# Issuing a kernel's first four loads between SyncE's arrival at the opening barrier and its wait there

## The chip, the cores and the metric

The kernel runs on one core of one Trainium2 chip. The metric is device time in microseconds (us) of one execution. A kernel is executed several times; a run is called slow when it lies over 1.5% above the fastest of the same kernel, and only fast runs are compared.

Two numbers are close but not the same. The *time* is what is compared. The *span* of a profile goes from the first to the last instruction that the profile shows.

## The reference

One decode step: conditioned layer norm, grouped-query attention over a cache of 8192 keys, then a gated MLP. Nearly all its bytes are weights and caches that are read once.

```python
# B=8, D=1024, Hq=32, Hkv=4, Sk=8192, Dh=128, F=3584, bfloat16
mod = silu(c) @ w_mod                     # (8, 6*1024): sa, ca, ga, sb, cb, gb
h = layernorm(x) * (1 + ca) + sa
x = x + ga * attention(h, k_cache, v_cache, wq, wo)
h = layernorm(x) * (1 + cb) + sb
x = x + gb * ((relu(h @ W_gate) * (h @ W_up)) @ W_down)
```

## The kernel before

All big operands pass through one ring in SBUF, the `arena`. A list of loads, in the order of use, is worked off by SyncE (SP in the profile); a load waits only until its part of the ring has been read by its last reader. Operations are recorded first and then emitted engine by engine, with a semaphore wait wherever another engine's result is needed.

```python
def pump():
    while stream:
        key, src, n = stream[0]
        lo = cursor[0] if cursor[0] + n <= RING else 0
        if P.unread("arena", lo, lo + n):
            return
        # ... (cut)
        P.op("sp", lambda e, dst=dst, src=src: e.dma_start(dst, src), writes=[slot_r(lo, lo + n)], dma=True)
# ... (cut)
for i in range(2):
    load(("wm", i), wm_src[:, 24 * D * i:24 * D * (i + 1)], 24 * D)        # w_mod, 2 x 6 MB
for i in range(2):
    load(("wq", i), wq_src[:, 2 * i * SLOT:2 * (i + 1) * SLOT], 2 * SLOT)  # 2 x 4 MB
for m in range(M):                                                         # 16 x (k, v), 4 MB each
    # ... (cut)
# ... then wo, W_gate and W_up, W_down in five parts, the last of 256 KB (cut)
head = stream[1:]
del stream[1:]
pump()                                     # load 1: first half of w_mod
for t, src in enumerate((c..., A_x...)):   # loads 2 and 3: c and x, 16 KB each (cut)
    P.op("sp", lambda e, t=t, src=src: e.dma_start(cx[:, t, :], src), writes=[R("cx", t, t + 1)], dma=True)
stream.extend(head)
P.pump = pump
pump()                                     # load 4: second half of w_mod; load 5: first half of wq; ...
```

The program opens with a barrier that the kernel's author did not write. Each of ACT, PE, DVE and SP has an instruction that signals its arrival and, right behind it, one that waits for the release. POOL first writes four constants, then waits for the four arrivals and releases everybody. All of the kernel's own instructions, loads too, come behind it.

## Time and profile before

| | before |
|---|---|
| time, median of the first 3 runs | 439.22 us (439.19 to 439.45) |
| time, mean of all 40 fast runs seen in this study | 439.52 us |
| share of the DMA engines' time that the loads take | 98.4% |
| first load issued after SP's arrival at the barrier | 0.74 us |

From the page of the kernel before: the span, the DMA engines' busy tenths in 40 equal slices, what they moved, three of the queues (packets, MB, share of 16 engines), the first being that of the loads, and the chain that ended last, by engine.

```profile
span 438.7 us, 4012 instructions
...
DMA  8999999999999999999999999999999999999994
GB/s 359 433 421 444 436 433 429 434 430 429 430 433 430 429 430 430 432 436 434 436 432 433 445 432 430 430 430 432 430 429 428 430 432 437 434 430 430 431 425 180
...
q1 hardware_dynamic: 6896, 185.64, 98.4%
q8 instruction: 13, 0.21, 0.2%
q14 instruction: 5, 0.04, 0.0%
...
PE 35%; DMA 32%; DVE 26%; ACT 4%; issue 2%; SPq 1%
...
```

The DMA row and the queue's 98.4% say that the DMA engines are the bound: they are at nine tenths or more in every slice but the first and the last, at about 430 GB/s. The last line must not be read as a list of costs. It is a walk back from the end, at each step to what released it; where a load waited on SP for its ring slot, the walk goes on through the matmul that freed it, however long the load then stood in the DMA queue.

The first 3 us of the timeline (columns: start, duration, engine, source line, operation, output and input):

```profile
...
0.34 0.10 POOL L641 MEMSET const-uint8-127<- 128x1 uint8 x1
0.73 1.28 ACT L292 ACT_TABLE_LOAD   x1 [0.73 <-PEq L641]
0.73 0.20 POOL L276 MEMSET identf<- 128x128 f32 x1 [0.29 <-POOLq L641]
0.74 0.40 SPq L237 DMA_DIRECT2D arena<-in_w_mod_dram  x1
...
1.19 0.42 SPq L266 DMA_DIRECT2D cx<-in_c_dram  x1
...
1.66 0.41 SPq L266 DMA_DIRECT2D cx<-in_A_x_dram  x1
...
2.11 0.67 SPq L237 DMA_DIRECT2D arena<-in_w_mod_dram  x1
2.82 0.51 SPq L237 DMA_DIRECT2D arena<-in_A_wq_dram  x1
```

Four constants of POOL, then the barrier, then everything else at once at 0.73 us: ACT loads its table, POOL goes on, and SP issues the first load at 0.74 us. A single row of "DMA_DIRECT2D" is the *issue* of a load, 0.4 us on SP's side, not its data. The Trainium skill says so ("Perfetto Trace Analysis", DMA Instruction — HWDGE): the movement of the data is not in the instruction's profiled window. The trace agrees: the issue is over at 1.14 us, the first packet of the load starts at 1.76 us and the load has landed at 18.5 us.

The instructions that the profile does not count as busy are in the trace as well. Here is the barrier, from the records of the trace (start and duration in us):

```
0.000 0.007 SP    arrives              0.534 0.017 POOL has all four arrivals
0.116 0.010 DVE   arrives              0.612 0.017 POOL releases
0.132 0.008 ACT   arrives              0.654 0.017 SP   passes
0.304 0.186 POOL  finishes constants   0.658 0.017 ACT  passes
0.316 0.008 PE    arrives              0.736 0.403 SP   issues load 1
```

SP is the first to arrive and has 0.65 us of waiting before it. What SP waited for in the whole program (total us, times, longest):

```profile
...
engine line waited for: us in total, times, longest us
SPq L237 <- PE ps L482: 201.6, 16, 13.3
...
SPq L641 <- PEq L641: 0.7, 1, 0.7
```

The barrier is the last line, 0.7 us. (The view puts it down to PE. In the records PE is the last of the four to arrive, and POOL, busy with its constants until 0.49 us, is the one that releases.) The other waits of loads (the longest is shown) are for ring slots; they are long, but loads already in the queue keep the DMA engines busy through them.

The end of the timeline: the last matmuls, the first of the two last DVE operations, SP's two stores:

```profile
...
434.86 1.02 PE L610 MATMUL ps<-arena,kt 128*32 128x256 bf16 x12 [0.18 <-DMA arena<-in_B_W_down_dram]
...
435.93 0.42 DVE L614 TENSOR_TENSOR lu<-ps,mod 128x256 f32<-128x256 f32 x1 [12.25 <-PE ps L610]
...
436.84 0.71 SPq L621 DMA_DIRECT2D out_dram<-ob  x2
...
```

### The profile page before, as it was taken

The page shows a single profiled execution, that of the slowest core. Times are in us where ns is not written, and L with a number is a line of the kernel's source. Part 1 is how long each engine was busy: PE and PEld are TensorE (multiplying, and loading weights), DVE is VectorE, ACT ScalarE, POOL GpSimd, SP SyncE. Part 2 cuts the span into 40 slices and gives each one's busy share as a digit, 9 for nine tenths or more (in the row PEclk, how much of TensorE's full clock was granted, in tenths as well). Part 3 has the DMA queues.
Part 4 walks back from the last instruction along what each step waited for, and adds up shares of the span by engine and source line. Part 5 has one row for each costly group of instructions (what it writes and reads, how often), then busy time and mean ns, then how long its engine had stood idle before and what let it go on. Part 6 is the DMA issues. An engine that isn't in the chain of part 4 may idle for free.

```text
span 438.7 us, 4012 instructions
## 1 busy us (share of the span) xinstructions
PE 271.6 (62%) x1691; PEld 121.2 (28%) x1691; DVE 263.6 (60%) x372; ACT 28.8 (7%) x48; POOL 19.8 (5%) x77
## 2 busy tenths in 40 slices
PE   0053446759595866859586776859586685655243
PEld 0021112324242332324233332424233242342021
DVE  0143057787687867778596867869687878430020
ACT  1100012010101011010101001010101101100000
POOL 6000010000000000000000000000000000000000
PEclk9997669697888969698796968888798978685556
DMA  8999999999999999999999999999999999999994
GB/s 359 433 421 444 436 433 429 434 430 429 430 433 430 429 430 430 432 436 434 436 432 433 445 432 430 430 430 432 430 429 428 430 432 437 434 430 430 431 425 180
DMA packets 6946, 185.90 MB, mean 424 GB/s; under 512 B 816, under 2 KB 912, under 8 KB 1168
## 3 DMA queue, kind: packets, MB, share of 16 engines
q1 hardware_dynamic: 6896, 185.64, 98.4%
q8 instruction: 13, 0.21, 0.2%
q14 instruction: 5, 0.04, 0.0%
q10 hardware_dynamic: 32, 0.01, 0.0%
HBM read 185.63 MB, written 0.02 MB: 423 GB/s over the span
## 4 chain that ended last, share of the span: by engine, by line
PE 35%; DMA 32%; DVE 26%; ACT 4%; issue 2%; SPq 1%
PE ps L482 18%; DMA arena<-in_A_k_cache_dram 15%; PE ps L439 13%; DVE kt L428 10%; DMA arena<-in_A_wq_dram 9%; DMA arena<-in_B_W_down_dram 8%; DVE pT L473 7%; DVE negm L446 4%; ACT prb L466 4%; PE ps L452 1%; PE ps L571 1%; DVE mj L457 1%; PE ps L375 1%; PE ps L592 1%; DVE mjt L460 1%
## 5 line engine op out<-in xcount | busy, mean ns | idle before, releaser
L428 DVE STREAM_TRANSPOSE kt<-arena 128x1024 uint32<-128x1024 uint32 x128 | 149.1, 1215 | 40.4 <-DMA arena<-in_A_k_cache_dram 33.1
L439 PE MATMUL ps<-kt,qpad 128*128 128x512 bf16 x512 | 120.8, 382 | 10.0 <-DVE kt L428 8.7
L482 PE MATMUL ps<-arena,pT 128*64 128x512 bf16 x512 | 94.0, 547 | 51.1 <-DVE pT L473 51.1
L482 PEld LDWEIGHTS ps<-arena,pT 128*64 128x64 bf16 x512 | 44.8, 155 | 94.5 <-issue 89.7
L439 PEld LDWEIGHTS ps<-kt,qpad 128*128 128x128 bf16 x512 | 45.5, 97 | 83.7 <-DVE kt L428 26.5
L473 DVE STREAM_TRANSPOSE pT<-prb 64x1024 bf16<-64x1024 bf16 x32 | 39.6, 1239 | 15.9 <-ACT prb L466 15.4
L466 ACT ACTIVATE prb<-ps,bias 128x1024 bf16<-128x1024 f32 x16 | 17.8, 1113 | 275.0 <-DVE mjt L460 275.0
L446 DVE TENSOR_REDUCE negm<-ps 128x1 f32<-128x512 f32 x32 | 22.1, 689 | 11.7 <-PE ps L439 11.7
L421 POOL COPY qpad<-qR 32x32 bf16<-32x32 bf16 x64 | 13.0, 203 | 308.2 <-PE ps L439 253.8
L592 PE MATMUL ps<-arena,hT 128*32 128x448 bf16 x128 | 12.7, 577 | 14.5 <-DMA arena<-in_B_W_up_dram 6.8
L452 PE MATMUL ps<-identf,negm 128*128 128x128 f32 x32 | 7.8, 325 | 15.7 <-DVE negm L450 15.7
L495 DVE SCALAR_TENSOR_TENSOR om<-ps,im,om 128x128 f32<-128x128 f32 x48 | 16.7, 347 | 0.6
L599 DVE TENSOR_TENSOR kt<-ps,kt 128x448 bf16<-128x448 f32 x2 | 1.2, 619 | 25.0 <-PE ps L592 25.0
L500 PE MATMUL ps<-jmp,om 128*128 128x16 f32 x32 | 6.5, 279 | 14.7 <-DVE om L495 14.7
L375 PE MATMUL ps<-arena,hT 128*32 128x512 bf16 x64 | 6.9, 608 | 13.9 <-DMA arena<-in_A_wq_dram 13.9
L290 DVE CAST cxr<-ps 128x512 bf16<-128x512 f32 x1 | 0.7, 692 | 19.6 <-PE ps L288 19.6
L288 PE MATMUL ps<-cx,rsel 32*128 32x512 bf16 x1 | 0.6, 581 | 19.0 <-DMA cx<-in_A_x_dram 19.0
L610 PE MATMUL ps<-arena,kt 128*32 128x256 bf16 x112 | 6.0, 372 | 9.2 <-DMA arena<-in_B_W_down_dram 9.2
L452 PEld LDWEIGHTS ps<-identf,negm 128*128 128x128 f32 x32 | 4.7, 186 | 23.6 <-DVE negm L450 22.1
L385 DVE CAST kt<-ps 128x512 bf16<-128x512 f32 x1 | 0.7, 692 | 17.2 <-PE ps L375 17.2
L592 PEld LDWEIGHTS ps<-arena,hT 128*32 128x32 bf16 x128 | 4.5, 139 | 22.0 <-DMA arena<-in_B_W_up_dram 8.4
L500 PEld LDWEIGHTS ps<-jmp,om 128*128 128x128 f32 x32 | 5.0, 195 | 18.0 <-DVE om L495 16.9
(80 smaller groups left out, 94.7 us busy)
## 6 DMA issues: line engine op xcount, KB each, us to landing
arena<-in_A_k_cache_dram SPq DMA_DIRECT2D x16, 4096.0 KB, 28.2
arena<-in_A_v_cache_dram SPq DMA_DIRECT2D x16, 4096.0 KB, 25.1
arena<-in_w_mod_dram SPq DMA_DIRECT2D x2, 6144.0 KB, 17.8
arena<-in_A_wq_dram SPq DMA_DIRECT2D x2, 4096.0 KB, 20.0
arena<-in_A_wo_dram SPq DMA_DIRECT2D x2, 4096.0 KB, 26.9
arena<-in_B_W_gate_dram SPq DMA_DIRECT2D x2, 3584.0 KB, 29.4
arena<-in_B_W_up_dram SPq DMA_DIRECT2D x2, 3584.0 KB, 32.5
arena<-in_B_W_down_dram SPq DMA_DIRECT2D x1, 3584.0 KB, 36.0
```

Source lines behind the costliest of these rows:

```text
L375: fns.append(lambda e, w=w, z=z, g=g, kk=kk: e.matmul(ps[32 * g:32 * g + 32, 3 + z, :], hT[:, kk, :], w[:, g, z, :], start=(kk == 0), stop ...
L421: P.op("pool", lambda e, n=2 * m + Q // 2, Q=Q: e.tensor_copy(qpad[32 * Q:32 * Q + 32, m % 2, :, 24 + 32 * Q:32 + 32 * Q], qR[32 * Q:32 * ...
L428: P.op("dve", lambda e: e.transpose(ktb[:, to:to + QE].bitcast(dt.uint32), arena[:, lo:lo + QE].bitcast(dt.uint32)), reads=[slot_r(lo, lo ...
L439: fns.append(lambda e, t=t, r=r: e.matmul(ps[:, b, :].rearrange("p (c k) -> p c k", k=32), qpad[:, m % 2, t * 2 + r, 24 - 8 * i:152 - 8 * ...
L446: P.op("dve", lambda e: e.tensor_reduce(negm[:, h:h + 1], ps[:, b, :], AX.X, ALU.max, negate=True), reads=[bank(b)], writes=[R("negm", h, ...
L452: P.op("pe", lambda e: e.matmul(ps[:, 4, 0:128], negm[:, 2:3].to_broadcast([128, 128]), identf[:], start=True, stop=True), reads=[R("negm" ...
L466: P.op("act", lambda e: e.activation(prb[:], ps[:, 2 * z:2 * z + 2, :].rearrange("p h n -> p (h n)"), ACT.Exp, bias=bias[:, z:z + 1], scal ...
L473: P.op("dve", lambda e, g=g: e.transpose(pT[64 * g:64 * g + 64, z, :, g, :], prb[64 * g:64 * g + 64, :]), reads=[R("prb"), R("pT", z, z + ...
L482: fns.append(lambda e, t=t: e.matmul(ps[64 * (t % 2):64 * (t % 2) + 64, 5, :].rearrange("p (i d) -> p i d", d=Dh), pT[:, z, t].rearrange(" ...
L495: P.op("dve", lambda e, i=i: e.scalar_tensor_tensor(out=om[:], in0=ps[:, 5, Dh * i:Dh * i + Dh], scalar=im[:, i:i + 1], in1=om[:], op0=ALU ...
L500: P.op("pe", lambda e: e.matmul(ps[:, 6, 16 * m:16 * m + 16], om[:], jmp[:].rearrange("p g j -> p (g j)"), start=True, stop=True), reads=[ ...
L592: fns.append(lambda e, w=w, r=kk - r0, kk=kk, h=h, j=j, b0=b0: e.matmul(ps[32 * j:32 * j + 32, b0 + h, 0:H], hT[:, kk, :], w[:, r, j, h, : ...
```

## The change

The intent is to use the 0.65 us that SP spends at the barrier. The recorded order of the kernel stays; after everything is emitted, the first four loads are moved, in the program's instruction list, from behind SP's wait to between its arrival and its wait.

```diff
+def start_loads_first(nc, n):
+    block = nc.main_func.blocks[0]
+    ins = list(block.instructions)
+    sp = [i for i, x in enumerate(ins) if x.engine == mybir.EngineType.SP]
+    at = next(i for i in sp if ins[i].opcode == "EventSemaphore")
+    first = [ins[i] for i in sp if i > at][:n]
+    assert all(x.opcode == "DMACopy" and not x.sync_info.on_wait for x in first), [x.opcode for x in first]
+    names = {x.name for x in first}
+    rest = [x for x in ins if x.name not in names]
+    at = next(i for i, x in enumerate(rest) if x.engine == mybir.EngineType.SP and x.opcode == "EventSemaphore")
+    block.instructions = rest[:at] + first + rest[at:]
 ... (cut)
             P.emit(name, e, sems)
+        start_loads_first(nc, 4)
```

No load waits for anything (the assertion holds it), and none writes a place that another instruction touches before the barrier.

## The prediction

> **What bounds the kernel now.** The DMA engines. In the 40-slice row they are 8-9 tenths busy everywhere but in the last slice. The page's queue table gives the loads' queue 98.4% of the span of 16 engines, 423 GB/s over the span; the window from 10 to 428 us has a DMA share of 1.00 and 431 GB/s. The Trainium skill ("DMA: Bandwidth & Descriptors", Specifications) gives a fabric ceiling of 435 GB/s, and the trace agrees within 1%; its 358 GB/s HBM limit for one core is not what this trace shows. PE (62%) and DVE (60%) are not the bound. The compute chain does decide when arena slots come free, but loads wait in the queue long after issue (median 25 to 36 us from issue to landing in the list of DMA issues, against some 10 us to move 4 MB), so the stream has about 15 us of slack against the consumers. Time is therefore: when the first byte starts + 185.6 MB at a fixed rate + a tail (last weights landing, last matmuls, two DVE operations, store; last weights landed by 435.4 us, end at 438.7 us).
>
> **What the change does.** Nothing is added or removed, and SP's order of loads is the same. Four loads (w_mod half 0, c, x, w_mod half 1) move ahead of SP's wait at the opening barrier. From the instructions of the first microsecond: SP arrives at the barrier at 0.000 us (it is the first; POOL, after its four constant memsets, collects the arrivals at 0.534 us and releases at 0.612 us), SP passes at 0.654 us, and the first load is issued at 0.736 us. The first packet starts at 1.76 us, 1.02 us after issue.
>
> After the change the first load should be issued some 0.05 to 0.1 us after SP's arrival (the gap after its barrier wait is now 0.08 us), so at about 0.07 us, with the first packet at about 1.1 us. Gain at the head: 0.736 - 0.07 = 0.66 us. The other engines are released as before, since SP's arrival is signalled ahead of its loads. SP's own wait comes about 2 us later, already satisfied; it costs the fifth load (wq half 0, now issued at 2.8 us) perhaps 0.1 us, and that load isn't needed by the queue before some 30 us.
>
> **How much is on the critical path.** All of it, once: the DMA stream is continuous, so it ends 0.66 us earlier and the tail follows. No feedback from compute: rsel and the other constants are ready many us before c and x land (17 to 19 us).
>
> **Predicted time:** 439.22 - 0.66 = 438.56 us; 438.2 to 439.0 holds it 8 times in 10 (the three runs of before spread 0.26 us). The effect is 0.15%: faster by over 2% 0.003, within 2% 0.994, slower by over 2% 0.003.
>
> **What would show it right or wrong in the profile.** First load's issue near 0.07 us on SP; first packet near 1.1 us; landings of w_mod half 0 (now 17.1 to 18.5 us), of the middle k and v loads and of the last W_down load each about 0.66 us earlier; the same 423-424 GB/s; barrier release of the other engines unchanged at about 0.66 us.
>
> **What would make it wrong.** (a) Issue to first packet grows, because the queue isn't ready so early: gain lost at the head. (b) The DMA stream's length changes by chance by as much as the gain (0.1% of 430 us is 0.43 us), which hides or doubles it in one run. (c) Stalls by slot release eat it: then landings keep their lead until some slot and lose it there. (d) The clock of the span starts at another instruction than SP's arrival, and the lead is not counted.

## The result, and the profile after

| | before | after |
|---|---|---|
| time, median of 6 runs | 439.34 us (439.16 to 446.05, one slow) | 439.01 us (438.62 to 439.20) |
| time, mean of the fast runs | 439.33 us (5 runs) | 438.95 us (6 runs) |
| ratio of the fast runs | | 0.9991, 95% interval 0.9979 to 1.0003 |

A ratio is the mean time of one kernel's fast runs over that of the other's fast runs of the same rounds, so it is not quite the ratio of the medians in the table. This first interval reaches 1: from these runs alone the gain is not proved.

The lines of the page that answer to those above:

```profile
span 437.3 us, 4012 instructions
...
DMA  9999999999999999999999999999999999999995
GB/s 382 426 439 433 432 432 430 429 432 430 435 432 432 433 438 432 434 432 435 429 430 438 435 430 435 435 435 430 432 430 432 435 430 426 433 434 426 438 420 208
...
q1 hardware_dynamic: 6896, 185.64, 98.7%
q8 instruction: 13, 0.21, 0.2%
...
PE 39%; DMA 28%; DVE 27%; ACT 4%; issue 2%; SPq 0%
...
```

The first 3 us of its timeline:

```profile
...
0.08 0.40 SPq L251 DMA_DIRECT2D arena<-in_w_mod_dram  x1
...
0.34 0.10 POOL L656 MEMSET const-uint8-127<- 128x1 uint8 x1
0.54 0.42 SPq L280 DMA_DIRECT2D cx<-in_c_dram  x1
0.73 1.28 ACT L306 ACT_TABLE_LOAD   x1 [0.73 <-PEq L656]
0.73 0.20 POOL L290 MEMSET identf<- 128x128 f32 x1 [0.29 <-POOLq L656]
1.00 0.42 SPq L280 DMA_DIRECT2D cx<-in_A_x_dram  x1
...
1.46 0.42 SPq L251 DMA_DIRECT2D arena<-in_w_mod_dram  x1
...
2.02 0.42 SPq L251 DMA_DIRECT2D arena<-in_A_wq_dram  x1
```

The load is issued at 0.08 instead of 0.74 us, the constants, ACT's table load and POOL's next work start where they did (0.73 us), and slice one moves 382 instead of 359 GB/s. The added lines moved the source lines down by 14 (the barrier's L641, behind the added call, by 15): L237 is now L251. SP's waits (the longest line alone; the barrier wait is no longer in the list, and the records show SP passing at 1.94 us, behind the four issues, without having to wait):

```profile
...
SPq L251 <- PE ps L496: 199.5, 16, 13.4
...
```

The end:

```profile
...
433.40 1.04 PE L624 MATMUL ps<-arena,kt 128*32 128x256 bf16 x12 [0.16 <-DMA arena<-in_B_W_down_dram]
...
434.49 0.42 DVE L628 TENSOR_TENSOR lu<-ps,mod 128x256 f32<-128x256 f32 x1 [11.31 <-PE ps L624]
...
435.40 0.71 SPq L635 DMA_DIRECT2D out_dram<-ob  x2
...
```

Here is something to be careful with. This pair of profiles says that the span fell from 438.7 to 437.3 us, 1.4 us, and that the last matmuls start 1.46 us earlier. The head accounts for 0.65 us of that. The timed runs say 0.4 to 0.6 us (means of the fast runs, here and in the repeat below). A trace keeps enough to see which is right: each load has 16 semaphore increments, the last load's spread over 2.6 to 4.1 us. They are read here as one from each of the 16 DMA engines as its share lands; no record names the engine, so this reading is an inference. The following table is worked out from the packets' starts and from these increments. "First done" and "last done" are the first and the last of the 16 DMA engines to be done with the last part of W_down, "lag" is their difference, "tail" is from there to the end of the span. All times in us, fast executions only; the runs are told in the next section.

```
run                issue  first packet  first done  last done  lag   tail  end     first done - first packet
before             0.74   1.76          431.35      435.43     4.08  3.30  438.73  429.59
control_before     0.74   1.76          431.33      434.90     3.56  3.30  438.19  429.57
after              0.08   1.11          430.66      433.99     3.33  3.31  437.30  429.55
repeat_change_2    0.08   1.09          430.70      433.97     3.27  3.31  437.27  429.61
cx_only            1.06   2.04          431.62      434.69     3.07  3.30  437.99  429.58
late_by_1          1.93   2.94          432.57      435.78     3.22  3.31  439.09  429.62
late_by_7          7.69   8.71          438.30      442.19     3.90  3.30  445.49  429.58
before_arrival     0.00   1.02          430.63      433.69     3.06  3.30  436.99  429.60
fewer_matmuls      0.08   1.09          430.66      433.29     2.63  3.30  436.59  429.57
```

The span is first packet + 429.6 + lag + 3.3. Two of the four terms never move, over nine executions: the stream of the least disturbed DMA engine takes 429.55 to 429.62 us, the tail 3.30 to 3.31 us. The head moves as it is moved. The lag scatters between 3.1 and 4.1 us among the eight executions with the same number of matmuls, and by half a microsecond between two of the very same program. The first trace of the kernel before happened to have the largest, and that is where the other 0.75 us of the 1.4 us come from (4.08 - 3.33). That first trace is also an unlucky execution as a whole: with the 1.3 us added its time would be 440.0 us, more than any of the three timed runs showed.

### The profile page after: what moved, and what is told of

Its sections match the earlier page's. It is cut to its first block, busy times and chain, and to the rows that moved or that the text cites. A ratio compares the mean times of both kernels' runs of the same rounds, so it can differ in the third digit from the quotient of the medians.

```text
span 437.3 us, 4012 instructions
## 1 busy us (share of the span) xinstructions
PE 272.1 (62%) x1691; PEld 121.2 (28%) x1691; DVE 263.8 (60%) x372; ACT 28.8 (7%) x48; POOL 19.8 (5%) x77
## 4 chain that ended last, share of the span: by engine, by line
PE 39%; DMA 28%; DVE 27%; ACT 4%; issue 2%; SPq 0%
PE ps L496 19%; PE ps L453 15%; DMA arena<-in_A_k_cache_dram 13%; DVE kt L442 10%; DVE pT L487 8%; DMA arena<-in_B_W_down_dram 8%; DMA arena<-in_w_mod_dram 7%; DVE negm L460 5%; ACT prb L480 4%; PE ps L466 2%; PE ps L585 1%; DVE mj L471 1%; PE ps L606 1%; PE ps L366 1%; DVE mjt L474 1%
## 5 line engine op out<-in xcount | busy, mean ns | idle before, releaser
L453 PE MATMUL ps<-kt,qpad 128*128 128x512 bf16 x512 | 122.1, 385 | 10.0 <-DVE kt L442 8.6
L496 PE MATMUL ps<-arena,pT 128*64 128x512 bf16 x512 | 92.0, 538 | 51.0 <-DVE pT L487 51.0
L624 PE MATMUL ps<-arena,kt 128*32 128x256 bf16 x112 | 6.9, 416 | 7.3 <-DMA arena<-in_B_W_down_dram 7.3
```

The lines of the kernel that those rows point to most:

```text
L453: fns.append(lambda e, t=t, r=r: e.matmul(ps[:, b, :].rearrange("p (c k) -> p c k", k=32), qpad[:, m % 2, t * 2 + r, 24 - 8 * i:152 - 8 * ...
L496: fns.append(lambda e, t=t: e.matmul(ps[64 * (t % 2):64 * (t % 2) + 64, 5, :].rearrange("p (i d) -> p i d", d=Dh), pT[:, z, t].rearrange(" ...
```

## The experiments

All were given five rounds each, beside the kernel before on the same chip. Theory A: the head counts once and in full, because the DMA stream is continuous from its first packet to its end. The rivals are named in the expectations.

### The change again (repeat_change)

No edit. Expected:

> The changed kernel again, to narrow the interval. Theory A (the head counts once, 0.65 us): mean of the rounds 0.5 to 0.8 us under the kernel before, 438.5 to 438.9 us; in the trace the first packet again near 1.1 us and the first-finishing DMA engine about 0.65 to 0.7 us ahead in every load, while the last-finishing engine's lead scatters between 0.4 and 1.5 us. Rival B (the gain is what the first pair of profiles shows, 1.4 us of span): time about 437.9 us. Rival C (the lead is lost later): no difference from the kernel before.

Measured: fast runs 438.51 to 439.18 us, mean 438.92; the kernel before 439.18 to 439.73, mean 439.52 (11 runs); ratio 0.9987 (0.9974 to 1.0000). The difference of the means is 0.60 us, as A expects, and B's 1.4 us is out: no run of the change reaches 437.9 us. The profiled run was slow (466.21 us), so its time can't be compared with the others. Its first packet was at 1.11 us like the others, but the stream of the first-done engine took 457.2 instead of 429.6 us, at an unlowered PE clock (0.815). A 4 MB load landed every 10.8 us instead of every 9.7 us until about 285 us, and every 9.7 us from then on. The slow trace of first_load_only shows the same until about 85 us (stream 436.7 us, clock 0.803). What slowed the data, no record tells.

### The kernel before against itself (control_before)

No edit. Expected:

> The kernel before against itself: ratio 1.000, and a second trace of it. Theory A with the remark that instruction fetches put single DMA engines back: the first packet again at 1.76 us, but the lag of the last-finishing engine behind the first at the last load differs from the first trace's 4.1 us by several tenths, and the span with it. If the 0.78 us of the two spans' difference that is not the head belongs to the change, the lag is again 4.1 us and the span 438.7.

Measured: ratio 1.0001 (0.9988 to 1.0013). The second trace of the same program has the first packet at 1.76 us again and the first engine done at 431.33 us (431.35 before), but a lag of 3.56 instead of 4.08 us and a span of 438.2 instead of 438.7. So the lag, and half a microsecond of the span, differ between executions of one program, as A's remark expects.

### The change once more (repeat_change_2)

No edit. Expected:

> The changed kernel once more, for five more rounds and a trace in the fast state. Theory A (head 0.65 us, once): mean 0.5 to 0.7 us under the kernel before, as in the first two comparisons together; trace with first packet at 1.1 us and the first-finishing DMA engine done with the last W_down load at 430.6 to 430.7 us (431.33 and 431.35 us in the two traces of the kernel before). The lag of the last-finishing engine is open: 3.1 to 4.1 us.

Measured: fast runs 438.58, 439.55, 438.55 and 439.33 us (one slow at 445.75), mean 439.00; before 439.69 (439.49 without one run at 441.64 that still counts as fast); ratio 0.9983 (0.9964 to 1.0003). The trace has the first packet at 1.09 and the first engine done at 430.70 us, as expected, with a lag of 3.27 us.

Over the whole study the change has 14 fast runs with a mean of 438.96 us and the kernel before 40 with 439.52: a difference of 0.56 us, with a 95% interval of 0.21 us to either side if the runs, which come from several chips, are taken as independent (0.51 us without the run at 441.64). No single comparison was narrow enough for that.

### The first load alone (first_load_only)

```diff
-        start_loads_first(nc, 4)
+        start_loads_first(nc, 1)
```

> Only the first load (6 MB of w_mod) moves ahead of the barrier wait; c, x and the second half stay behind it. Theory A: the stream is continuous from its first packet and the first load alone takes 14 us, so the gain is the same as with four loads: within 0.2 us of the repeat of the change. Rival D (c and x, which start the compute chain, are what counts): the gain shrinks, as c and x are issued at about 0.75 and 1.2 us instead of 0.54 and 1.0.

Measured: fast runs 438.70 to 439.13 us, mean 438.87, 0.65 us under the kernel before's 439.52 and within 0.05 us of the repeat in the same rounds; ratio 0.9985 (0.9973 to 0.9998). Its profiled run was slow, but the head can be read from it: load 1 is issued at 0.08, c at 0.73 and x at 1.12 us. One moved load gives the whole gain; the other three, as moved, are worth nothing that can be seen.

### c and x alone (cx_only)

```diff
-    first = [ins[i] for i in sp if i > at][:n]
+    first = [ins[i] for i in sp if i > at][1:1 + n]
-        start_loads_first(nc, 4)
+        start_loads_first(nc, 2)
```

> Only c and x (16 KB each) move ahead of the barrier wait; the big load follows behind it, after their two issues: c at about 0.08, x at 0.54, w_mod half 0 at about 1.07 us instead of 0.74. Theory A (what counts is when the big stream starts): no gain, but a loss of 0.3 us against the kernel before, about 439.8 us, although four input rows arrive 15 us earlier; first packet of the big load near 2.1 us. Rival D (an early c and x start the compute chain earlier and that counts): faster than the kernel before by 0.5 us or more.

From the first 3 us of its timeline:

```profile
...
0.08 0.38 SPq L280 DMA_DIRECT2D cx<-in_c_dram  x1
...
0.52 0.41 SPq L280 DMA_DIRECT2D cx<-in_A_x_dram  x1
...
1.06 0.83 SPq L251 DMA_DIRECT2D arena<-in_w_mod_dram  x2
...
1.94 0.43 SPq L251 DMA_DIRECT2D arena<-in_A_wq_dram  x1
...
2.21 0.58 PE L302 MATMUL ps<-cx,rsel 32*128 32x512 bf16 x1 [2.21 <-DMA cx<-in_A_x_dram]
...
```

c and x are issued at 0.08 and 0.52 us, and the first matmul of the compute chain runs at 2.21 us, instead of about 19 us in the kernel before. It buys nothing: fast runs 439.32 to 439.82 us, mean 439.62, ratio 0.9999 (0.9981 to 1.0017). Rival D is out. The expected loss of 0.3 us is not resolved by the timed runs. The trace has it: the big load is issued at 1.06 us, its first packet starts at 2.04 and the first engine is done at 431.62 us, 0.28 us later than in the kernel before.

### Everything later by 1.2 and by 7 us (late_by_1, late_by_7)

The recording of POOL's constants is moved ahead of that of the loads, and SP is made to wait for one of them before its first load.

```diff
+        P.op("sp", [], reads=[R("rsel")])       # late_by_7: R("identb")
         head = stream[1:]
         del stream[1:]
         pump()
```

> A dose of the size of the change, in the other direction: all loads wait for POOL's copy of rsel (done at 1.89 us), so the first is issued at about 1.95 instead of 0.74 us. Theory A: +1.1 to +1.3 us over the kernel before, about 440.7 us. Rival C (slack in the ring absorbs small shifts of the head, only large ones show): within 0.4 us of the kernel before.

> The opposite dose: all loads wait for POOL's last constant (done at 7.67 us), the first load is issued at about 7.7 us instead of 0.74. Theory A (every microsecond of the head counts once): time +6.9 to 7.1 us over the kernel before, about 446.2 us; first packet near 8.7 us; first-finishing engine late by about 7.0 us at every load. Rival C (slack downstream absorbs a shift of the head): clearly less than +6.5 us.

Measured: late_by_1, three fast runs 440.39, 440.64 and 440.80 us (three slow), mean 440.61, 0.92 us over the kernel before (1.12 us without its run at 441.64); ratio 1.0020 (0.9998 to 1.0041), so its timed runs alone don't prove the loss. late_by_7: 446.38, 446.67, 446.82 and 448.53 us, median of these four 446.74 (one slow); 7.2 us over the median of before (439.57). Ratio 1.0173 (1.0157 to 1.0188); it is a ratio of means and holds the run at 448.53. In the traces the first packet came 1.18 and 6.95 us later than in the kernel before, and the first engine was done 1.23 and 6.96 us later. So from -0.65 to +7 us the shift at the head is found whole at the end of the stream. Rival C, that slack downstream absorbs it, is out. The run at 448.53 us is not explained; it has no trace.

### Fewer matmuls (fewer_matmuls)

On top of the change, a wrong result on purpose. It asks where the lag comes from.

```diff
-            for t in range(2):
-                for r in range(2):
+            for t in range(1):
+                for r in range(1):                 # scores: 1 of 4 matmuls, stop=(i == 3)
-            for t in range(32):
+            for t in range(16):                    # values: 16 of 32 matmuls, stop=(t >= 14)
```

The pages of before and after count 13 packets on queue q8, of the kind "instruction", and their records have 16 KB each.

The Trainium skill ("Runtime: NRT & Kernel Launch", Instruction fetch mechanics) says that each engine's instruction memory is refilled in blocks of 16 KiB, 256 instructions, by a DMA queue of the sequencer's own, and that crossing a block costs one bump, mostly hidden. PE's 1691 matmuls and 1691 weight loads are 3382 instructions; over 256 that is 13.2 (an estimate with the page's figure), and 13 packets are there. In all traces looked at, the lag grows near these packets and hardly between them: summed over the 15 other engines, the lag behind the first-done one grows from 3.5 us after the second half of w_mod to 26.2 us at the last load in repeat_change_2, 1.75 us for each of the 13 fetches, if all of it is put down to them (1.73 in the profile after, 1.74 in control_before). Not all of it is theirs: every trace also has the five packets on q14, 8 KB each, and the lag grows near these too. A fit of the growth to the number of packets of each kind gives 1.5 us for one of q8 and 0.7 for one of q14 in the profile after, 1.4 and 0.8 in repeat_change_2.

> On top of the change, wrong result on purpose: a quarter of the score matmuls and half of the value matmuls, 640 matmuls and as many weight loads less, same loads of data. Theory E (PE's instruction fetches, 16 KB each, set single DMA engines back by 1.65 us of engine time each, and the last-finishing engine ends the stream): 13 fetches become about 8, the lag of the last-finishing engine at the last W_down load falls from 3.1-4.1 us to under 3 us, and the time falls by 0.4 to 1.0 us against the change. Rival F (the lag is a trait of certain DMA engines or of the data stream): lag and time as with the change, within 0.2 us.

From its page: the span, the busy times, the queues of loads and of instructions, and the chain by engine.

```profile
span 436.6 us, 2732 instructions
...
PE 197.3 (45%) x1051; PEld 75.1 (17%) x1051; DVE 260.7 (60%) x372; ACT 28.8 (7%) x48; POOL 19.9 (5%) x77
...
q1 hardware_dynamic: 6896, 185.64, 98.8%
q8 instruction: 8, 0.13, 0.1%
q14 instruction: 5, 0.04, 0.0%
...
DMA 72%; DVE 21%; PE 5%; ACT 0%; issue 0%; SPq 0%
...
```

Eight fetches, as expected; a lag of the last engine of 2.63 us instead of 3.27 and 3.33; a summed lag of 19.1 instead of 26.2 us, so 1.4 us for each fetch less, under the 1.65 us of the expectation, which counted q8 alone, and in line with the fit (1.4 and 0.7 us in this trace too); the other three terms of the sum unchanged (first packet 1.09, stream 429.57, tail 3.30 us). The time is 437.91 to 438.11 us, mean 438.01, 0.95 us under the mean of the change, at the upper end of what E expected, and the runs spread by 0.2 instead of 1.0 us. (The lags of the traces account for 0.6 to 0.7 us of the 0.95; the profiled executions of the change were among its fastest.) Theory F is out, as far as this goes: fewer PE instructions bring fewer fetches and less lag. The edit also took away PE work, and no run took away fetches alone, so PE's share in the time, rather than the fetches', remains as an objection; against it stand the unchanged stream and tail. What decides which DMA engine takes a fetch is open: no record here tells the engines apart.

The page answers a second question. PE's busy time fell from 272.1 to 197.3 us and its place in the chain from 39% to 5%, and the time fell by 0.2%. The chain's PE share was no cost.

Between 10 and 428 us, first this kernel, then the profile after, last the kernel before (columns: stretch, length, busy time and count of PE, PEld, DVE, ACT and POOL, granted PE clock, DMA share, GB/s):

```profile
...
core 0: us, PE busy (x) PEld busy (x) DVE busy (x) ACT busy (x) POOL busy (x), PEclk, DMA share, GB/s
10.00:428.00 418.00, 193.53 (x995) 73.45 (x995) 259.84 (x370) 27.51 (x47) 13.07 (x64) 0.59 1.00 432
...
```

```profile
...
10.00:428.00 418.00, 267.75 (x1631) 119.42 (x1635) 262.98 (x370) 27.51 (x47) 13.00 (x64) 0.81 1.00 432
...
```

```profile
...
10.00:428.00 418.00, 267.70 (x1619) 119.35 (x1623) 262.76 (x370) 27.50 (x47) 13.01 (x64) 0.81 1.00 431
...
```

With fewer matmuls the granted clock was 0.59 instead of 0.81 (0.59 to 0.61 in all five runs), and 38% of the matmuls less (640 of 1691) took away only 27% of the busy time; the lower clock is a likely reason, not a tested one. The DMA share and rate did not notice.

### The first load ahead of the arrival (before_arrival)

```diff
-    at = next(i for i, x in enumerate(rest) if x.engine == ... SP and x.opcode == "EventSemaphore")
+    at = next(i for i, x in enumerate(rest) if x.engine == ... SP and x.opcode == "Drain")
-        start_loads_first(nc, 4)
+        start_loads_first(nc, 1)
```

("Drain" is SP's arriving instruction.)

> The first load alone is issued ahead of SP's arrival at the barrier, not just ahead of its wait there; its issue takes 0.40 us, so SP arrives at about 0.45 us, still ahead of POOL (0.53 us), and nobody is released later. Theory A: the load can be earlier by only the 0.08 us between arrival and first load, so first packet at about 1.02 to 1.05 us after the span's first instruction, time within 0.2 us of the change (about 438.9 us) and about 0.6 us under the kernel before. If the time's own clock started at SP's arrival, the time would fall by a further 0.4 us.

From the first 3 us of its timeline:

```profile
...
0.00 0.41 SPq L251 DMA_DIRECT2D arena<-in_w_mod_dram  x1
...
0.80 1.28 ACT L306 ACT_TABLE_LOAD   x1 [0.80 <-PEq L656]
...
0.81 0.34 SPq L280 DMA_DIRECT2D cx<-in_c_dram  x1
...
```

Measured: first packet at 1.02 us, first engine done at 430.63 us, time 438.22 to 439.23, mean 438.75; ratio 0.9987 (0.9972 to 1.0001) to the kernel before. The last 0.07 us of the head are taken, and the trace has them, but the runs can't tell this kernel from the change (438.96), so it is not called faster. The expectation was wrong in one point: SP's arriving instruction ran at 0.458 us for 0.121 us (0.007 before), POOL got the four arrivals at 0.605 instead of 0.534 us, and everybody was released 0.07 us later. It cost nothing here, since the first matmul, which needs POOL's constants, waits for c and x until about 18 us. The time's own clock does not start at SP's arrival: the time is again 1.3 us above the span, which now begins with the load.

## Why the prediction was right, point by point

- *The DMA engines are the bound.* Right. The window from 10 to 428 us has a DMA share of 1.00 with and without the change, and the strongest case is the kernel with 640 matmuls less: 0.95 us. The mean rate over the span was forecast unchanged at 423 to 424 GB/s; the page says 425, the same bytes in a shorter span.
- *First load at about 0.07 us, first packet at about 1.1 us.* Right: 0.08 and 1.11 us. From issue to first packet it took 1.03 us instead of 1.02; the queue was ready that early, so (a) of the ways to be wrong did not happen.
- *The others are released as before.* Right: ACT's table load at 0.73 us in both.
- *SP's own wait about 2 us later costs the fifth load perhaps 0.1 us.* SP passes at 1.94 us and the wait took 0.02 us; the fifth load goes out at 2.02 instead of 2.82 us. It was known not to matter.
- *All of it on the critical path, once.* Right, and shown in both directions: the first-done engine's end follows the first packet with 429.55 to 429.62 us between them, from a head of 1.02 to one of 8.71 us. So (c) did not happen, and (d) not either: time less span is 1.3 us throughout.
- *The size, 0.66 us.* The means of all fast runs differ by 0.56 us (0.35 to 0.77), the traces' heads by 0.65 us.
- *Each landing about 0.66 us earlier.* Right for the first engine of each load (0.55 to 0.73 us over the whole trace), not for the last one, which is what a consumer waits for: 0.43 to 1.46 us. The prediction had not thought of a load as 16 shares with their own delays. Its (b), a chance of about 0.4 us in one run, had the right size, but the wrong place: it is not the length of the stream that varies, it is the lag of its last engine.
- *438.56 us.* The median measured is 439.01, at the very end of the range (438.2 to 439.0) and 0.45 us above the point, an error two thirds as large as the effect. That the range held it is a matter of hundredths, so luck in part. The larger part of the error is the number it was subtracted from: the first three runs of the kernel before have a median of 439.22, 40 runs a mean of 439.52. A gain of 0.66 us taken from there would be 438.86 us.

## What to carry to other kernels

If a kernel's loads stream without a gap as here, expect the time between the start of the program and the first packet of the first large load to count in full; and a load that waits for nothing can be issued while its engine would only stand at a barrier; the two small loads that start the compute chain counted for nothing here, since the chain was not the bound. For effects under a microsecond don't read the difference of two spans: split the span into head, stream, lag of the last DMA engine and tail, and see which of them moved. Three runs of the kernel before are too few to subtract half a microsecond from.

## What the Trainium skill lacked or had wrong

- "Runtime: NRT & Kernel Launch", Instruction fetch mechanics: it calls the crossing of a 16 KiB block "mostly hidden" and says nothing of what a fetch costs the loads of a kernel bound by DMA. Here a fetch is a 16 KB packet of about 0.9 us; with 8 instead of 13 the lags of the DMA engines, added up, fell from 26.2 to 19.1 us and the kernel was 0.95 us shorter, 0.2 us for each fetch if all of it is put down to them, which is not shown.
- "DMA: Bandwidth & Descriptors", Latency and other measured facts: it notes that some DMA engines are usually slower, with a guess that holds for DMAs issued by POOL alone. Here all loads are issued by SP, and still the last of the 16 engines ended 2.6 to 4.1 us after the first, differently from execution to execution of one program. Which engines were last, no record tells.
- The same page, same section, gives about 600 ns to the first byte for loads from SP or ACT, and does not say from when it counts. From the end of the issue to the first packet it was 0.61 to 0.63 us in all eleven traces, which agrees; from the start of the issue, which is what a head is made of, it was 0.97 to 1.03 us.
- The same page, Specifications, lists 358 GB/s as the HBM limit of one core, half of a stack's 716, beside a fabric ceiling of 435, and does not say when which holds (the page does under Bandwidth: 358 is for both cores of a pair streaming). This program's one core streamed 431 to 432 GB/s between 10 and 428 us; the ceiling is the figure that held.
- No page was found on a one-core kernel in which the data come slower at an unlowered PE clock: 457.2 and 436.7 instead of 429.6 us for the same stream, clocks 0.815 and 0.803; a 4 MB load every 10.8 instead of 9.7 us for a part of the run.
- No page was found for what an arrival at a barrier costs behind a load's issue: 0.121 us instead of 0.007, in the one trace that has it.
